# One group of P matmuls for w1 and w2 in every second slot, and attention's matmuls in those slots

## The chip, the cores and the metric

The kernel runs on one core of one Trainium2 chip. The metric is the device time of one execution in microseconds (us), the median of several runs. Of the core's engines, TensorE (PE in the profile, with PEld for its weight loads) does the matmuls, VectorE (DVE) and ScalarE (ACT) read their results out of PSUM and do all elementwise work, GpSimd (POOL) helps at the end, and SyncE (SP) issues DMAs.

## What is computed

All data are 32-bit floats. An attention block with a small state is followed by two feed-forward blocks:

```python
# x: (8, 8, 512, 64), state: (8, 8, 32, 64); softmax over the last axis, scale = 1/8
xread = softmax(scale * x @ state.T) @ state
sread = softmax(scale * state @ x.T) @ x
y = concatenate([xread, sread], axis=2)          # per batch: 544 rows of 8 * 64 = 512
h = ((y @ w1) * (y @ w2)) @ w3 @ w_out           # w1, w2: 512 x 1024, w3: 1024 x 1024, w_out: 1024 x 512
t = h @ w_in                                     # w_in: 512 x 2048
out = (t * clip(t + 3, 0, 6) / 6) @ w_out2       # w_out2: 2048 x 512
```

## The kernel before

**Stages.** A first stage converts w_out, w3, w1 and w2 from their raw words, 20 units of 1024 columns in the order of the string `ORDER` (L120). It multiplies w3 by w_out once (the tiles w3p), and `more` (L666) places the first attention and the first matmuls of the next stage between the units. The second stage goes over the eight batches b, each in eight slots (`slot`, L625), one for every 128 columns of w1 and w2. The third stage does the last two lines of the reference with a Strassen scheme, 33 rounds; it takes more than half of the time and the change does not touch it.

**P.** A slot needs y @ w1 and y @ w2 for 512 rows. The xread half of y is a product a @ state, so the kernel multiplies state by 256 columns of w1 or w2 first. The result is P, and the slot multiplies a with P. `p_mm(v, i)` (L346) makes P for two slots (pair v = 4 b + m // 2), for w1 (i = 0) or w2 (i = 1), with eight small matmuls of 64 rows by 32 columns in plain 32-bit form, which the trace shows as 16 instructions, into two PSUM banks (c = 0, 1), of which each fills 256 of 512 columns. `p_split(v, i)` (L361) then splits each bank into a rounded part (ph, ACT) and a rest (pl, DVE), because the large matmuls work on rounded operands in three terms: `mm3` (L87) is rounded by rounded, and the two mixed terms.

**A slot.** PE's order in slot m is written out by hand: two banks `ps_ab0` and `ps_ab1` (a with P for w1, then for w2, six matmuls each), then in `x2_one` (L534) six matmuls into the accumulators x2 for the slot two before, then what `mid_` (L741) issues, then six more for x2. On ACT and DVE, `ab_mul` (L500) copies ps_ab0 (asb) and multiplies ps_ab1 with it (ab); `ab_hi` and `ab_lo` split ab (abh, abl). `mid_` calls `p_mm` and `p_split` for the next pair, w1 in even slots and w2 in odd ones, and one step of the attention for batch b + 1. Another step of it is taken before (`before`, L736). After that, DVE and ACT do two steps of `stream2` (L422), which converts and splits the weights of the third stage.

**Attention.** `attention(b)` (L182) is a generator; each `yield` ends a step. For b from 2 on (`fine` is false) it takes steps in 16 places of the eight slots. Four of its parts put matmuls on PE: `scores` (two groups, ps_s), `e2_t` (two groups of transposes, ps_e), and `sread` (ps_r). In the kernel before these fall in the middles of slots 0, 1, 3, 4 and 5. The DVE parts are `scores_out`, `max_n`, `sum_n`, `div_n` and `turn`; `exp_n` is ACT's. `sread_out` copies the state's result (xs) and stores it with a DMA on SP; after batch 7's the stored rows are loaded again as xs_r, rounded on ACT (xs_h), and multiplied in `s_block` (L557), ahead of the last batch's slots.

**Banks.** The matmuls of slots, P and attention share four PSUM banks (`bank`, L66). A bank is handed out again in the order in which the last readers of the banks stand in the program. The order of each engine's queue is that of the program text.

Of the kernel before, what the change touches and what calls it, by code (L numbers as in the profile page):

```python
# [19 lines left out]
def attn_moe_kernel(tc, xt_d, xn_d, bd_d, wa, wb, wc, wi, wo, out):  # L20
# [18 lines left out]
    nc = tc.nc  # L39
# [26 lines left out]
    def bank(name):  # L66
        return psum.tile([128, 512], F32, tag="b", name=name, bufs=4)
# [114 lines left out]
    def attention(b, fine=False):  # L182
# [10 lines left out]
        def scores(g):  # L193

            ps = bank("ps_s")
            for j in range(2):
                c = 2 * g + j
                nc.tensor.matmul(ps[64 * j:64 * j + 64], br[:, c, :], xr[:, c, :], start=True, stop=True)  # L198
            return ps

        def scores_out(g, ps):
            nc.vector.tensor_reduce(out=m2[:, g:g + 1], in_=ps, op=ALU.max, axis=AX.X)
            nc.vector.tensor_scalar(out=m2[:, g:g + 1], in0=m2[:, g:g + 1], scalar1=-scale, scalar2=None, op0=ALU.mult)
            nc.vector.transpose(out=sN[:, g, :], in_=ps)
            nc.scalar.activation(out=e2[:, g, :], in_=ps, func=AF.Exp, bias=m2[:, g:g + 1], scale=scale,
                                 accum_out=r2[:, g:g + 1])
# [58 lines left out]
        if fine:  # L265
            ps = scores(0)
            yield
            scores_out(0, ps)
            yield
            ps = scores(1)  # L270
            yield
            scores_out(1, ps)
        else:
            scores_out(0, scores(0))
            yield
            yield
            scores_out(1, scores(1))
        yield
        max_n()
        yield  # L280
        exp_n()
        yield
        e2t = att.tile([128, T, 2, 128], F32, tag="xtl", name="e2t")
        sm = att.tile([128, 32, 1], F32, tag="sm", name="sm", bufs=2)
        if fine:
            ps = e2_t(0)
            yield
            e2_out(0, ps)
            sum_n()
            yield  # L290
            ps = e2_t(1)
            yield
            e2_out(1, ps)
            div_n()
            yield
            ps = sread()
            yield
            sread_out(ps)
            aT = att.tile([128, 2, 512], F32, tag="e2", name="aT")
            turn(aT)  # L300
        else:
            sum_n()
            yield
            e2_out(0, e2_t(0))
            yield
            div_n()
            yield
            e2_out(1, e2_t(1))
            yield
            aT = att.tile([128, 2, 512], F32, tag="e2", name="aT")  # L310
            turn(aT)
            yield
            sread_out(sread())
        yield
        pool = late if b % 2 else mid
        A_h = pool.tile([128, 2, 512], F32R, tag="Ah", name="Ah")
# [2 lines left out]
        rnd(A_h, aT, "A")  # L319
        yield  # L320
        rest(A_l, aT, A_h, "V")

    live = []

# [11 lines left out]
    with tc.manual_schedule():  # L336
# [6 lines left out]

        p_ps, phl = {}, {}

        def p_mm(v, i):  # L346
            b, mm = divmod(v, 4)
            ps = p_ps[v, i] = [bank("ps_p") for c in range(2)]
            o = 512 * i + 256 * (mm % 2)

            for q in range(4):
                for c in range(2):
                    j, k = divmod(q, 2)
                    r = slice(64 * (k ^ c), 64 * (k ^ c) + 64)
                    nc.tensor.matmul(ps[c][32 * q:32 * q + 32, :256], st_t[b][r, 2 * c + j, 32 * k:32 * k + 32],  # L355
                                     w12[mm // 2, 2 * c + j][r, o:o + 256], start=True, stop=True)

        def p_tile(hl):
            return main.tile([128, 512], F32R, tag=f"p{hl}", name=f"p{hl}", bufs=4)

        def p_split(v, i):  # L361
            ps = p_ps.pop((v, i))
            h, l = p_tile("h"), p_tile("l")
            h, l = phl[v, i] = h.rearrange("p (c k) -> p c k", c=2), l.rearrange("p (c k) -> p c k", c=2)
            for c in range(2):
                rnd(h[:, c], ps[c][:, :256], "A")
            for c in range(2):
                rest(l[:, c], ps[c][:, :256], h[:, c], "V")

        def w3_out(m, ps):  # L370
            w3p_h[m], w3p_l[m] = w3p_tile("h", m), w3p_tile("l", m)
# [294 lines left out]
        def more(t):  # L666
            if t == 1 or t == 8:
                load_x(t // 8)
            if t in (4, 16):
                live.append(attention(t // 16, True))  # L670
                step()

            for _ in range({5: 1, 6: 1, 7: 1, 8: 1, 10: 1, 11: 1, 12: 2, 13: 1, 17: 1, 18: 1, 19: 1}.get(t, 0)):
                step()
            for m in {9: (0, 1), 10: (2, 3), 12: (4,), 14: (5,), 17: (6,), 18: (7,)}.get(t, ()):
                w3_done(m)
            if 15 <= t <= 17 or t == 19:
                ab = ab_mul(*e_ps.pop(min(t - 15, 3)), 512)
            for v in {14: ((0, 0), (0, 1)), 15: ((1, 0),), 16: ((1, 1),)}.get(t, ()):
                p_split(*v)  # L680
            if 15 <= t <= 17 or t == 19:
                hi = ab_hi(ab, 512)
                e_ab[min(t - 15, 3)] = hi, ab_lo(ab, hi, 512)

            if 14 <= t <= 17:
                early_mm(t - 14)
            for v in {13: ((0, 0), (0, 1)), 14: ((1, 0),), 15: ((1, 1),), 19: ((2, 0), (2, 1))}.get(t, ()):
                p_mm(*v)
            if t in (4, 5, 9, 10, 11, 16, 17):
                step()  # L690
            if ORDER[t] in "aw":
                w3u[ORDER[:t].count("a") + ORDER[:t].count("w")].mm()
            bulk_mm(4)
            if t == 18:
                early_x2(0)
                early_x2(1)
            if t == 19:
                early_x2(2)
                step()
# [4 lines left out]
        close_pool("cv")  # L704
        late = open_pool("late", bufs=1, side=left, reuse_waits="tile")
        cvs = open_pool("cvs", bufs=1, side=right, reuse_waits="tile")
        for i in range(2):
            p_split(2, i)
        early_x2(3)
        second = stream2()  # L710
        for b in range(B):
# [20 lines left out]
            for m in range(0 if b else 4, M1):  # L732
                if m == (6 if b else 7) and b + 2 < B:
                    load_x(b + 2)

                def before():  # L736
                    step()

                vn, i = 4 * b + m // 2 + 1, m % 2

                def mid_():  # L741
                    if vn < 4 * B:
                        p_mm(vn, i)
                        p_split(vn, i)
                    step()
                slot(b, m, A, before, mid_)
                if b == 0:
                    step()
                for _ in range(STEPS):
                    next(second, None)  # L750
                if b == B - 2 and m >= 3:
                    ws_split(m - 3)
                if b == B - 1:
                    if m == 0:
                        x2_load(0)
                    else:
                        next(first, None)
                        next(first, None)
# [282 lines left out]
```

## Time and profile before

| | us |
|---|---|
| median of 3 runs | 1289.04 (1288.55 to 1289.30) |
| the profiled execution | 1290.92 |
| its span, first to last instruction | 1289.1 |
| TensorE busy in it | 1249.1 (97%) |
| VectorE busy | 863.7 (67%) |
| ScalarE busy | 525.1 (41%) |
| second stage, first slot to last | about 116 to 566 |

The span is cut into windows; for each the profile gives the busy time of each engine and the clock that TensorE was granted, 1.00 being full. A matmul's own duration overlaps with that of the next, so that the cost of one is read from the distance of two starts. "Idle before" is the time in which an engine had nothing to do, with the instruction that ended it.

### The profile page before, as it was taken

How to read it: one execution, taken by the hardware profiler on the slowest of the kernel's cores; microseconds unless marked ns; L12 is line 12 of the kernel's file. 1: busy time of each engine (PE TensorE's matmuls, PEld its weight loads, DVE VectorE, ACT ScalarE, POOL GpSimd, SP SyncE). 2: the span in 40 equal slices, each digit the busy share in tenths (PEclk: the TensorE clock that was granted, in tenths of full speed). 3: DMA queues.
4: the chain of work that ended last, by engine and by line, in shares of the span. 5: the costliest groups of instructions: out<-in, count | busy, mean ns of one | idle time of the engine just before them, and what ended most of it. 6: DMA issues, size and time to landing. Idle time of an engine off the chain costs nothing.

```text
span 1289.1 us, 16960 instructions
## 1 busy us (share of the span) xinstructions
PE 1249.1 (97%) x6784; PEld 966.8 (75%) x6784; DVE 863.7 (67%) x1332; ACT 525.1 (41%) x875; POOL 32.2 (2%) x18
## 2 busy tenths in 40 slices
PE   5979999999999999999999999999999999999997
PEld 2446676777767778787888888888888888888886
DVE  7976777786777652545757846668557686655663
ACT  3433546454655543434323443334433254332330
POOL 0000000000000000000000200002000020000000
PEclk9989999999999999999999999999999999999999
DMA  9741555555455200346334562535634344242223
GB/s 362 267 163 66 202 187 192 199 188 194 178 187 180 99 19 34 111 159 238 138 131 156 197 223 93 180 103 190 236 140 154 117 178 173 105 160 95 90 90 114
DMA packets 49590, 202.68 MB, mean 157 GB/s; under 512 B 9192, under 2 KB 11240, under 8 KB 42856
## 3 DMA queue, kind: packets, MB, share of 16 engines
q1 hardware_dynamic: 48936, 200.56, 43.3%
q8 instruction: 53, 0.87, 0.3%
q10 hardware_dynamic: 576, 1.05, 0.2%
q14 instruction: 25, 0.20, 0.0%
HBM read 160.17 MB, written 41.42 MB: 156 GB/s over the span
## 4 chain that ended last, share of the span: by engine, by line
PE 86%; DVE 8%; ACT 3%; DMA 1%; issue 1%; ACTq 0%; DVEq 0%; SPq 0%
PE ps L801 23%; PE ps_o L88 10%; PE ps_o L90 10%; PE ps_o L89 10%; PE x L88 5%; PE ps_ab L88 4%; PE x L90 4%; PE x L89 4%; PE ps_ab L90 4%; PE ps_ab L89 4%; PE ps_p L355 2%; PE ps_hs L801 2%; PE ps_r L228 1%; PE ps_s L198 1%; PE ps_sb L90 1%
## 5 line engine op out<-in xcount | busy, mean ns | idle before, releaser
L801 PE MATMUL ps<-xc,wh 128*128 128x512 f32 x896 | 276.7, 390 | 0.0
L805 DVE TENSOR_TENSOR oa<-oa,ps_o 128x512 f32<-128x512 f32 x238 | 163.2, 687 | 166.3 <-PE ps_o L90 165.7
L88 PE MATMUL ps_o<-woh,g 128*128 128x512 f32 x512 | 203.4, 397 | 0.4 <-ACT g L71 0.4
L90 PE MATMUL ps_o<-woh,g 128*128 128x512 f32 x512 | 201.9, 394 | 0.0
L89 PE MATMUL ps_o<-wol,g 128*128 128x512 f32 x512 | 201.5, 394 | 0.0
L801 PEld LDWEIGHTS ps<-xc,wh 128*128 128x128 f32 x896 | 168.3, 188 | 36.3
L801 PE MATMUL ps<-xc,wl 128*128 128x512 f32 x448 | 175.7, 392 | 0.0
L71 ACT ACTIVATE g<-gt 128x512 fp32r<-128x512 f32 x128 | 81.1, 634 | 177.7 <-DVE gt L815 177.6
L88 PE MATMUL x<-abh,w3ph 128*128 128x512 f32 (+1 forms) x288 | 115.7, 402 | 0.0
L90 PEld LDWEIGHTS ps_o<-woh,g 128*128 128x128 f32 x512 | 96.3, 188 | 23.8 <-DVE g L79 0.4
L89 PEld LDWEIGHTS ps_o<-wol,g 128*128 128x128 f32 x512 | 97.0, 189 | 21.4
L88 PEld LDWEIGHTS ps_o<-woh,g 128*128 128x128 f32 x512 | 96.4, 188 | 21.5 <-ACT g L71 0.8
L90 PE MATMUL x<-abh,w3pl 128*128 128x512 f32 (+1 forms) x288 | 109.3, 379 | 0.0
L89 PE MATMUL x<-abl,w3ph 128*128 128x512 f32 (+1 forms) x288 | 109.1, 379 | 0.0
L88 PE MATMUL ps_ab<-Ah,ph 128*128 128x512 f32 x256 | 102.6, 401 | 5.3 <-DVE pl L79 5.2
L79 DVE TENSOR_TENSOR g<-gt,g 128x512 fp32r<-128x512 f32 x128 | 89.7, 701 | 18.7 <-ACT g L71 16.3
L90 PE MATMUL ps_ab<-Ah,pl 128*128 128x512 f32 x256 | 100.4, 392 | 0.0
L89 PE MATMUL ps_ab<-Al,ph 128*128 128x512 f32 x256 | 100.3, 392 | 0.0
L801 PEld LDWEIGHTS ps<-xc,wl 128*128 128x128 f32 x448 | 84.1, 188 | 18.2
L504 DVE TENSOR_TENSOR ab<-ps_ab,asb 128x512 f32<-128x512 f32 x64 | 44.1, 689 | 60.5 <-PE ps_ab L90 41.0
L71 ACT ACTIVATE abh<-ab 128x512 fp32r<-128x512 f32 (+1 forms) x72 | 43.8, 608 | 98.2 <-DVE ab L504 98.2
L812 ACT ACTIVATE rl<-c,half 128x512 f32<-128x512 f32 x96 | 69.4, 723 | 32.4 <-DVE c L805 30.9
(122 smaller groups left out, 1752.3 us busy)
## 6 DMA issues: line engine op xcount, KB each, us to landing
wh<-swih SPq DMA_DIRECT2D x33, 896.0 KB, 4.6
wl<-swil SPq DMA_DIRECT2D x33, 896.0 KB, 6.4
woh<-swoh SPq DMA_DIRECT2D x33, 512.0 KB, 5.5
wol<-swol SPq DMA_DIRECT2D x33, 512.0 KB, 6.6
out_dram<-oa SPq DMA_DIRECT2D x34, 256.0 KB, 2.4
raw<-in_wb_dram SPq DMA_DIRECT2D x8, 1024.0 KB, 7.1
xr<-in_xt_dram SPq DMA_DIRECT2D x8, 1024.0 KB, 6.5
xn<-in_xn_dram SPq DMA_DIRECT2D x8, 1024.0 KB, 7.1
```

What stands on the lines that cost most here:

```text
L71: nc.scalar.activation(out=out_, in_=in_, func=AF.Copy)
L79: e.tensor_tensor(out=out_, in0=in_, in1=hi.bitcast(F32), op=ALU.subtract)
L88: nc.tensor.matmul(ps, lh, rh, start=first, stop=False)
L89: nc.tensor.matmul(ps, lh, rl, start=False, stop=False)
L90: nc.tensor.matmul(ps, ll, rh, start=False, stop=last)
L198: nc.tensor.matmul(ps[64 * j:64 * j + 64], br[:, c, :], xr[:, c, :], start=True, stop=True)
L228: nc.tensor.matmul(ps[h:h + 64, c * NS:(c + 1) * NS], xn[:, t, c * 128 + h:c * 128 + h + 64], e2t[:, t, g, o:o + NS], start=(t == 0), stop ...
L355: nc.tensor.matmul(ps[c][32 * q:32 * q + 32, :256], st_t[b][r, 2 * c + j, 32 * k:32 * k + 32], w12[mm // 2, 2 * c + j][r, o:o + 256], star ...
L504: nc.vector.tensor_tensor(out=ab[:, :n], in0=psb[:, :n], in1=a[:, :n], op=ALU.mult)
L801: nc.tensor.matmul(ps, u[:, a, k, :], v[:, k, :], start=first and k == 0 and i == 0, stop=k == 1 and i == 2, skip_group_check=not first or ...
L805: nc.vector.tensor_tensor(out=out_, in0=a, in1=b, op=ALU.add)
L812: nc.scalar.activation(out=rl, in_=c, func=AF.Relu, bias=half, scale=1.0 / 6.0)
```

## The change

P for w1 and w2 of a pair is made by one call, in even slots only: 16 matmuls (32 instructions) into the same two banks, w1 in columns 0 to 255 and w2 in columns 256 to 511. The splits take 512 columns at a time, two on ACT and two on DVE for a pair instead of four and four; the tiles ph and pl are twice as wide and half as many. Attention's steps for `fine` false are placed anew: both `scores` groups in the middle of slot 0, both `e2_t` groups in the middle of slot 4, `sread` in the middle of slot 6, each behind P on PE; `max_n` goes to slot 1, `exp_n` ahead of the splits of slot 2, `div_n` to slot 3. In the first stage the three P pairs that are made there get one call each, with two banks instead of four.

```diff
             yield
             scores_out(1, ps)
         else:
-            scores_out(0, scores(0))
-            yield
-            yield
-            scores_out(1, scores(1))
+            ps = [scores(g) for g in range(2)]
+            for g in range(2):
+                scores_out(g, ps[g])
+            yield
         yield
         max_n()
         yield
         exp_n()
         yield
+        if not fine:
+            yield
...
             sum_n()
             yield
-            e2_out(0, e2_t(0))
-            yield
             div_n()
             yield
-            e2_out(1, e2_t(1))
+            yield
+            ps = [e2_t(u) for u in range(2)]
+            for u in range(2):
+                e2_out(u, ps[u])
             yield
             aT = att.tile([128, 2, 512], F32, tag="e2", name="aT")
             turn(aT)
-            yield
-            sread_out(sread())
...
         rest(A_l, aT, A_h, "V")
+        if not fine:
+            yield
+            sread_out(sread())
...
-        def p_mm(v, i):
+        def p_mm(v):
             b, mm = divmod(v, 4)
-            ps = p_ps[v, i] = [bank("ps_p") for c in range(2)]
-            o = 512 * i + 256 * (mm % 2)
...
+            ps = p_ps[v] = [bank("ps_p") for c in range(2)]
+
+            for i in range(2):
+                o = 512 * i + 256 * (mm % 2)
+                for q in range(4):
+                    for c in range(2):
+                        j, k = divmod(q, 2)
+                        r = slice(64 * (k ^ c), 64 * (k ^ c) + 64)
+                        nc.tensor.matmul(ps[c][32 * q:32 * q + 32, 256 * i:256 * i + 256],
+                                         st_t[b][r, 2 * c + j, 32 * k:32 * k + 32],
+                                         w12[mm // 2, 2 * c + j][r, o:o + 256], start=True, stop=True)
+
+        def p_split(v):
+            ps = p_ps.pop(v)
+            h, l = (main.tile([128, 2, 512], F32R, tag=f"p{hl}", name=f"p{hl}", bufs=2) for hl in "hl")
+            for i in range(2):
+                phl[v, i] = h[:, :, 256 * i:256 * i + 256], l[:, :, 256 * i:256 * i + 256]
             for c in range(2):
-                rnd(h[:, c], ps[c][:, :256], "A")
+                rnd(h[:, c], ps[c], "A")
             for c in range(2):
-                rest(l[:, c], ps[c][:, :256], h[:, c], "V")
+                rest(l[:, c], ps[c], h[:, c], "V")
...
-            for v in {14: ((0, 0), (0, 1)), 15: ((1, 0),), 16: ((1, 1),)}.get(t, ()):
-                p_split(*v)
+            if t in (14, 15):
+                p_split(t - 14)
...
-            for v in {13: ((0, 0), (0, 1)), 14: ((1, 0),), 15: ((1, 1),), 19: ((2, 0), (2, 1))}.get(t, ()):
-                p_mm(*v)
+            if t in (13, 14, 19):
+                p_mm({13: 0, 14: 1, 19: 2}[t])
...
-                vn, i = 4 * b + m // 2 + 1, m % 2
+                vn = 4 * b + m // 2 + 1
 
                 def mid_():
-                    if vn < 4 * B:
-                        p_mm(vn, i)
-                        p_split(vn, i)
+                    if vn < 4 * B and m % 2 == 0:
+                        p_mm(vn)
+                        p_split(vn)
                     step()
```

## Rows read from the trace of the kernel before

**Rows 1.** The page, part 4: the chain that ended last, by engine.

```profile
PE 86%; DVE 8%; ACT 3%; DMA 1%; issue 1%; ACTq 0%; DVEq 0%; SPq 0%
```

**Rows 2.** Busy time by window: PE, PEld, DVE, ACT, POOL, then clock, DMA share.

```profile
188.00:244.00 56.00, 54.80 (x401) 39.97 (x400) 42.50 (x71) 29.03 (x55) 0.00 (x0) 1.00 0.56 197
566.00:1289.00 723.00, 714.01 (x3190) 586.70 (x3189) 465.18 (x695) 260.24 (x398) 31.50 (x12) 1.00 0.43 152
```

**Rows 3.** Waits of PE: total us, how many times, the longest.

```profile
PE ps_ab L88 <- DVE pl L79: 5.2, 2, 4.2
...
PE ps_e L213 <- ACT asb L502: 2.7, 4, 1.2
...
PE ps_p L355 <- DVE ab L504: 1.4, 1, 1.4
```

**Rows 4.** PE in order of time (start, duration): a slot with P alone.

```profile
214.50 0.39 PE L89 MATMUL x<-abl,w3ph 128*128 128x512 f32 x1
214.73 0.39 PE L90 MATMUL x<-abh,w3pl 128*128 128x512 f32 x1
215.04 0.66 PE L355 MATMUL ps_p<-big,br 64*32 64x256 f32 x16
215.64 0.50 PE L88 MATMUL x<-abh,w3ph 128*128 128x512 f32 x1
215.97 0.39 PE L89 MATMUL x<-abl,w3ph 128*128 128x512 f32 x1
```

**Rows 5.** The same view, first stage: two P groups follow each other.

```profile
107.87 0.66 PE L355 MATMUL ps_p<-big,br 64*32 64x256 f32 x16
...
108.33 0.59 PE L355 MATMUL ps_p<-big,br 64*32 64x256 f32 x2
...
110.92 0.50 PE L88 MATMUL x<-abh,w3ph 128*128 128x512 f32 x1
```

**Rows 6.** The same view: P ahead of a scores group; transposes ahead of P.

```profile
119.23 0.60 PE L213 MATMUL ps_e<-ident,e 128*128 128x128 f32 x4
119.76 0.66 PE L355 MATMUL ps_p<-big,br 64*32 64x256 f32 x16
...
207.78 0.66 PE L355 MATMUL ps_p<-big,br 64*32 64x256 f32 x16
208.37 1.08 PE L198 MATMUL ps_s<-xr,br 128*64 128x512 f32 x4
```

**Rows 7.** Groups of instructions by shape: busy us, mean ns, idle before.

```profile
L79 DVE TENSOR_TENSOR pl<-ps_p,ph 128x256 fp32r<-128x256 f32 x128 | 47.9, 418 | 7.4 <-ACT ph L71 7.2
...
L504 DVE TENSOR_TENSOR ab<-ps_ab,asb 128x512 f32<-128x512 f32 x64 | 44.1, 689 | 60.5 <-PE ps_ab L90 41.0 <-ACT asb L502 19.2
...
L241 DVE TENSOR_TENSOR sN<-sN,mx 128x1024 f32<-128x1024 f32 x8 | 9.8, 1226 | 0.3
...
L79 DVE TENSOR_TENSOR w3pl<-ps_w,w3ph 128x512 fp32r<-128x512 f32 x8 | 5.3, 685 | 4.5 <-ACT w3ph L71 4.5
...
L71 ACT ACTIVATE w3ph<-ps_w 128x512 fp32r<-128x512 f32 x8 | 4.5, 596 | 0.0
```

**Rows 8.** Batch 7's state rows: issue and rounding in time; median landings.

```profile
462.15 0.32 SPq L723 DMA_DIRECT2D xs_r<-xsd  x1
...
473.89 1.05 ACT L71 ACTIVATE xs_h<-xs_r 128x1024 fp32r<-128x1024 f32 x1
...
xsd<-xs SPq DMA_DIRECT2D x8, 64.0 KB, 2.1
xs_r<-xsd SPq DMA_DIRECT2D x1, 512.0 KB, 3.3
```

**Rows 9.** PE alone by window: busy, instructions, granted clock.

```profile
223.10:224.60 1.50, 1.42 (x8) 1.00 0.79 330
...
477.90:480.30 2.40, 2.40 (x14) 0.50 0.00 0
```

**Rows 10.** DVE in order of time, end of the first stage.

```profile
111.03 0.69 DVE L79 TENSOR_TENSOR abl<-ab,abh 128x512 fp32r<-128x512 f32 x1 [0.76 <-ACT abh L71]
```

More of the change, by code (lines that the diff above doesn't have):

```diff
@@ L344, in attn_moe_kernel @@
         p_ps, phl = {}, {}
-        def p_mm(v, i):
+        def p_mm(v):
             b, mm = divmod(v, 4)
-            ps = p_ps[v, i] = [bank("ps_p") for c in range(2)]
-            o = 512 * i + 256 * (mm % 2)
[L351 to L364, printed above, removed]
+            ps = p_ps[v] = [bank("ps_p") for c in range(2)]
[13 more added lines that the diff above has]
+                phl[v, i] = h[:, :, 256 * i:256 * i + 256], l[:, :, 256 * i:256 * i + 256]
             for c in range(2):
-                rnd(h[:, c], ps[c][:, :256], "A")
+                rnd(h[:, c], ps[c], "A")
             for c in range(2):
-                rest(l[:, c], ps[c][:, :256], h[:, c], "V")
+                rest(l[:, c], ps[c], h[:, c], "V")
         def w3_out(m, ps):
@@ L706, in attn_moe_kernel @@
         cvs = open_pool("cvs", bufs=1, side=right, reuse_waits="tile")
-        for i in range(2):
-            p_split(2, i)
+        p_split(2)
         early_x2(3)
```

## The prediction

> **What bounds the kernel now.** I read the chain that ended last first: 86% of it is TensorE [rows 1]. The busy times by window say where: in one batch of the second stage PE is busy 54.80 of 56.00 us while DVE has 42.50, and in the third stage 714 of 723 [rows 2]. So time can be won in the second stage and ahead of it only, and in two ways: PE's few waits, or PE's own work made shorter. The list of waits is short: 5.2 us in all on the rest of P, of which 4.2 in one place of the first stage, 2.7 in four waits of the transposes for a ScalarE copy, 1.4 once where P waits for a bank [rows 3]. The rest must come from the busy time. The number of P's matmuls and their columns stay, so the third view is PE in order of time, around P, where a busy engine can be seen to lose time between matmuls.
>
> **What going into P and out of it costs.** Large matmuls start 0.23 us apart (214.50 to 214.73). P alone in a slot stretches L90 at 214.73 to the second matmul behind P, L89 at 215.97, to 1.24 us; two ordinary steps would be 0.46, so P costs 0.78 [rows 4]. P's own work is less. In the first stage two groups follow each other, and the second begins 0.46 us after the first (107.87 to 108.33) [rows 5]. So 16 instructions take 0.46, and 0.78 - 0.46 = 0.32 is lost on entering and leaving. The losses can be seen: P starts 0.31 behind a large matmul instead of 0.23, and the two matmuls behind P start late as well [rows 4].
>
> **The merged P.** A pair of slots now costs 2 x 0.78 = 1.56, and will cost 0.32 + 2 x 0.46 = 1.24: 0.32 less. There are 24 such pairs in batches 1 to 6 and 3 in batch 7 (pair 32 does not exist): 27 x 0.32 = 8.6 us, all of it on PE, which sets the end. Bounds: 0.25 to 0.40 a pair (the rows are rounded to 0.01, and four starts enter), 6.8 to 10.8.
>
> **Attention's groups.** Each of the five matmul groups now follows a P, so moving them adds no entry so long as every one sits behind a P; in slots 0, 4 and 6 it does. Two of the five, the second scores group and the second transposes, then follow a group of their own kind. The change from P to scores costs about 0.59 - 0.46 = 0.13 (207.78 to 208.37), that from transposes to P happens in 0.53 for four of them [rows 6]. I take 0.1 for each of the two, 6 batches: 1.2 us; bounds 0 (nothing is saved between equal groups) and 0.13 x 12 = 1.6.
>
> **Waits that go, and waits that come.** The transposes waited 2.7 us for the ScalarE copy because `exp_n` stood ahead of it; they move from slots 3 and 4 to slot 4 alone, a slot and a half after `exp_n`, so I take this wait as gone. What comes: with two banks for P and two for a pair of attention groups in the same slot, the banks come round differently. In slot 4, P takes the pair of slot 3, the transposes take slot 4's own ps_ab banks, and slot 5's ps_ab0 takes the bank that DVE's first pl frees. Count from the end of slot 4's ps_ab matmuls: six x2 matmuls (1.4), P (1.05 to the next group), two groups of transposes (1.0), six x2 (1.4) put slot 5's ps_ab0 at 4.8. DVE's part begins 0.2 later, since a matmul of 0.39 ends 0.2 after the start of the next [rows 4], and before that bank is free come ab 0.69, ACT's abh (0.6), abl 0.69 and the first pl, now 512 columns at 0.69 instead of 256 at 0.42 [rows 7]: 2.7. So DVE may enter slot 4 up to 1.9 us late; each us beyond that is a us of PE in each batch. The ACT splits (0.60 for 512 columns [rows 7]) fit between. The transposes' second bank waits for slot 4's ab, with about the same limit.
>
> How late is DVE? An odd slot lasts 24 x 0.23 = 5.5 us without P. In slot 1 DVE has ab, abl (1.4), `max_n` (two passes of 1024 columns at 1.23 [rows 7]) and at most two such passes of weight conversion: 6.3, late by 0.8. Slot 3 has `sum_n` and `div_n` instead: the same. Slot 0 has 8.3 of DVE work (both `scores_out` take 3.0) in about 8.6, but its pl must wait for P and the split, so it ends about 1 late; slot 2, 6.7 long with 5.2 of DVE work, makes up 1.2. That is 0.8 + 1.0 - 1.2 + 0.8 = 1.4 late at slot 4, between 1.0 (shorter conversion steps) and 2.6 (nothing made up in slot 2, where `exp_n` on ACT now stands ahead of abh and the splits). Cost per batch 0 to 0.7; I take 0.3, near the low end since 1.4 is below 1.9: 6 x 0.3 = 1.8. Net of both: 0.9 us gained, bounds +2.7 and 2.7 - 4.2 = -1.5. What is queued behind the ACT part of `exp_n` in slot 2 is abh, whose abl PE wants only two slots later, so there is cover of over 5 us.
>
> **The first stage.** P of pair 2 needs two free banks, not four. The wait of 1.4 falls away, since the bank it waited for is not taken. P starts at 107.87; the next x2 matmul then comes at 107.87 + 0.46 + 0.60 (P to x2 [rows 4]) = 108.93 instead of 110.92 [rows 5]: 2.0 us. The batch of x2 matmuls that follows must not overtake abl, which ends at 111.72 [rows 10]; twelve matmuls from 108.93 end at 111.7, so it is just in time, and I take 1.9. Around 72 us the wait of 4.2 for pl stays, because DVE is the late one there; a merged P for pair 1 gives 0.3 more and the freed banks let two matmuls go early. I take 0.5. Sum 2.4, bounds 1.0 (the chain of DVE gets there first) and 3.0. In batch 0, whose attention is the finer one, two pairs merge, but slot 5's `sread` still pays an entry of its own, and P of 32 instructions pushes one wait for pl (1.0 of the 5.2) back by about 0.5: I take 0.4 gained, bounds -0.5 and 0.9.
>
> **The state rows.** `sread` of batch 7 moves one slot later, and with it the copy, the store and the load of xs_r on SP. Now xs_r is issued at 462.15 and lands 3.3 later, at 465.5, but is used at 473.89 [rows 8]: 8 us of cover. In the new order the store comes about 3.3 us into slot 6's second half, 6.6 before the end of slot 7; 2.1 + 3.3 of landing [rows 8] fit into that, barely. 0, bounds -1.5 and +0.4. Behind it on SP stand only weight loads and stores with two units of lead; the load of the next x now stands ahead of it and waits for nothing late.
>
> **Sum.** 8.6 + 1.2 + 0.9 + 2.4 + 0.4 + 0 = 13.5 us. The profiled execution took 1290.92, its span 1289.1; it lies 0.15% above the median of 1289.04, and a difference carries over as it is: 1289.0 - 13.5 = 1275.5. All good ends together (10.8 + 1.6 + 2.7 + 3.0 + 0.9 + 0.4 = 19.4) give 1269.6, all bad ends (6.8 + 0 - 1.5 + 1.0 - 0.5 - 1.5 = 4.3) 1284.7.
>
> **Rivals.**
> *DVE is late in slot 4.* Against it: 13 us of each batch are free on DVE [rows 2]. For it: this slack lies in even slots where DVE now waits longer for the longer splits. Price: 1 us per batch for each us beyond 1.9. It eats the gain of 15.3 (the sum without the waits of 1.8 that I count) when DVE is 1.9 + 15.3 / 6 = 4.4 late, and at 5 late the time is 1289.0 - 15.3 + 6 x 3.1 = 1292.3, slower. That takes two more conversion passes in each batch's slots 1 to 3 than I counted. Chance of slower by this 0.07; of a part of it, 3 late and 1289.0 - 15.3 + 6.6 = 1280.3, 0.10.
> *No loss to save.* If the 0.32 belonged to every 16 instructions of P, not to the change of kind, the 8.6 and 1.2 would fall away: 1275.5 + 9.8 = 1285.3. Against it stands the distance of 0.46 between two groups, but that second group was cut off by a wait after two instructions [rows 5]. Chance 0.07; here the change leaves the cost of P as it was and does not do what it says.
> The page "TensorEngine Tiling (Array Packing)" of the Trainium skill (Tiling Modes, Key Properties) says that a change of tiling mode, unlike a change of tile, drains TensorE, which speaks against this rival; the 0.32 around P's 64 by 32 tiles agrees [rows 4], and the page gives no price.
> *The clock.* Longer stretches of small matmuls could lower TensorE's granted clock. Now it is 1.00 around a wait and a transposes group; after the gap ahead of `s_block` 14 matmuls ran at 0.50 (1.2 GHz) in 2.40 us [rows 9], half of which is lost. Once in each of 6 batches, twice over: 14 us, 1289.9, no change. Chance 0.03.
> The page "TensorE: Matmul & The Clock Gate" of the Trainium skill (Part 4) says that PE transposes don't count as busy for the gate, which speaks for this rival; the clock of 1.00 at the transposes [rows 9] speaks against it.
>
> **How the numbers follow.** Forecast as worked out: 0.73; the rivals 0.17, 0.07 and 0.03. The likeliest gives 1275.5. The range goes from 1270.0 to 1285.5: it holds the forecast to nearly all its ends, the half-late DVE and the case of no loss to save. Differences of 0.2% (2.6 us) are about what a measurement of this kernel can tell from none. Faster 0.87, the same 0.05, slower 0.08.
>
> **What would show it.** Right: in an odd slot PE shows no P, x2 matmuls 0.23 apart throughout; in an even slot 32 P instructions, and about 1.05 us from P's start to the next group; batches 1 to 6 shorter by 1.3 to 1.9 us each; the wait for ab in the first stage gone. Wrong: PE waits for pl or ab at ps_ab in slot 5 or at ps_e in slot 4, some us per batch; or 1.2 us and more for the second 16 instructions; or a granted clock under 1.00 inside a batch.

## The result, and the profile after

The changed kernel takes 1275.27 us (median of 4 runs, 1273.91 to 1276.16), the kernel before beside it 1289.17 (4 runs, 1288.55 to 1289.43). The ratio is 0.9892, with a 95% interval from 0.9877 to 0.9907: 13.9 us faster, where 13.5 were forecast. The profiled execution took 1276.16 us and its span 1274.1, against 1290.92 and 1289.1 before, so the two traces differ by 15.0 us. That is what is taken apart here.

What was said of P is seen first, in PE in order of time (start, duration, engine and line, operation, tile, count). An even slot of batch 5 in the changed kernel:

```profile
373.07 0.39 PE L90 MATMUL x<-abh,w3pl 128*128 128x512 f32 x1
373.39 1.09 PE L360 MATMUL ps_p<-big,br 64*32 64x256 f32 x32
374.41 0.50 PE L88 MATMUL x<-abh,w3ph 128*128 128x512 f32 x1
374.75 0.40 PE L89 MATMUL x<-abl,w3ph 128*128 128x512 f32 x1
```

Here 32 instructions stand between two large matmuls where [rows 4] have 16. P begins 0.32 us behind L90, and L88 1.02 behind P: forecast were 0.31 and 1.05. The odd slot behind it shows only large matmuls, 0.23 apart.

A slot's length is the distance of its first ps_ab matmul to that of the next slot. For batch 5, in us, from the PE starts of each trace (slots 0, 2, 4 and 6 are the even ones):

| slot | 0 | 1 | 2 | 3 | 4 | 5 | 6 | 7 |
|---|---|---|---|---|---|---|---|---|
| before | 7.29 | 7.27 | 6.25 | 6.67 | 6.67 | 8.28 | 6.28 | 6.27 |
| changed | 8.56 | 5.44 | 6.69 | 5.44 | 7.51 | 5.46 | 8.67 | 5.46 |

A slot without P or attention now lasts 5.44. P for one operand cost 6.25 - 5.44 = 0.81, P for both costs 6.69 - 5.44 = 1.25, so a pair saves 2 x 0.81 - 1.25 = 0.37. The two scores groups cost 1.04 + 1.00 before over a slot with P alone (6.25 in slot 2, 6.27 in the odd slot 7), and 8.56 - 6.69 = 1.87 now: 0.17 saved. The two transposes groups cost 0.40 + 0.42 before and 0.82 now: nothing.

Second, PE's waits in the changed kernel (total us, how many, the longest), which answer to [rows 3]:

```profile
PE ps_e L213 <- DVE ab L508: 2.5, 3, 1.1
PE ps_ab L90 <- DVE pl L79: 2.1, 1, 2.1
...
PE ps_ab L88 <- ACT ph L71: 1.1, 1, 1.1
PE ps_sb L89 <- DVE xs_l L79: 1.1, 1, 1.1
PE ps_ab L88 <- DVE pl L79: 0.9, 1, 0.9
```

The transposes' wait for ScalarE is gone, and so is P's wait for ab. A new wait has come: the transposes wait for DVE's ab, three times. The other lines on pl and ph are the first stage and batch 0; that on xs_l is `s_block`, with the same 1.1 before.

Third, one batch and the third stage by window (columns as in [rows 2]):

```profile
188.00:241.00 53.00, 52.06 (x395) 39.54 (x394) 41.32 (x62) 29.22 (x47) 0.00 (x0) 1.00 0.55 197
556.00:1274.00 718.00, 709.02 (x3168) 582.22 (x3166) 465.23 (x695) 258.93 (x396) 31.49 (x12) 1.00 0.43 152
```

PE is still busy nearly throughout, at clock 1.00; the batch is shorter because PE's own work is, and the third stage is as busy as it was [rows 2]. By stretch, from the starts of the slots (batch 0's slots 0 to 3 have their ps_ab matmuls in the first stage, so that its first slot here is slot 4):

| stretch | before | changed | gained |
|---|---|---|---|
| start to first slot of batch 0 | 116.51 | 115.47 | 1.0 |
| batch 0 | 23.68 | 23.01 | 0.7 |
| batches 1 to 5 | 278.57 | 269.97 | 8.6 |
| batch 6, slots 0 to 6 | 48.70 | 47.77 | 0.9 |
| its slot 7 and `s_block` | 51.99 | 49.40 | 2.6 |
| batch 7, seven slots | 40.48 | 39.29 | 1.2 |

The sum is 15.0. Batches 1 to 5 take 53.23, 54.61, 54.81, 54.09 and 53.23 us now; the middle three hold the new waits.

### The profile page after: what moved, and what is told of

Its sections match the earlier page's. It is cut to its first block, busy times and chain, and to the rows that moved or that the text cites. A ratio compares the mean times of both kernels' runs of the same rounds, so it can differ in the third digit from the quotient of the medians.

```text
span 1274.1 us, 16840 instructions
## 1 busy us (share of the span) xinstructions
PE 1237.6 (97%) x6784; PEld 972.2 (76%) x6784; DVE 858.0 (67%) x1268; ACT 518.7 (41%) x811; POOL 32.2 (3%) x18
## 3 DMA queue, kind: packets, MB, share of 16 engines
q10 hardware_dynamic: 576, 1.05, 0.2%
## 4 chain that ended last, share of the span: by engine, by line
PE 85%; DVE 9%; ACT 2%; DMA 1%; issue 1%; ACTq 0%; DVEq 0%; SPq 0%
PE ps L804 24%; PE ps_o L88 10%; PE ps_o L90 10%; PE ps_o L89 10%; PE x L88 4%; PE x L89 4%; PE x L90 4%; PE ps_ab L88 4%; PE ps_ab L90 4%; PE ps_ab L89 4%; PE ps_p L360 2%; PE ps_hs L804 2%; PE ps_w L414 1%; PE ps_r L228 1%; DVE ab L508 1%
## 5 line engine op out<-in xcount | busy, mean ns | idle before, releaser
L88 PE MATMUL ps_o<-woh,g 128*128 128x512 f32 x512 | 203.3, 397 | 0.3 <-ACT g L71 0.3
L90 PE MATMUL ps_o<-woh,g 128*128 128x512 f32 x512 | 201.8, 394 | 0.0
L89 PE MATMUL ps_o<-wol,g 128*128 128x512 f32 x512 | 201.4, 393 | 0.0
L90 PEld LDWEIGHTS ps_o<-woh,g 128*128 128x128 f32 x512 | 96.3, 188 | 23.8 <-DVE g L79 0.4
L89 PEld LDWEIGHTS ps_o<-wol,g 128*128 128x128 f32 x512 | 96.9, 189 | 21.5
L88 PEld LDWEIGHTS ps_o<-woh,g 128*128 128x128 f32 x512 | 96.4, 188 | 21.6 <-ACT g L71 0.8
L88 PE MATMUL x<-abh,w3ph 128*128 128x512 f32 (+1 forms) x288 | 112.3, 390 | 0.0
L89 PE MATMUL x<-abl,w3ph 128*128 128x512 f32 (+1 forms) x288 | 109.0, 378 | 0.0
L90 PE MATMUL x<-abh,w3pl 128*128 128x512 f32 (+1 forms) x288 | 108.8, 378 | 0.0
L88 PE MATMUL ps_ab<-Ah,ph 128*128 128x512 f32 x256 | 102.7, 401 | 2.0 <-ACT ph L71 1.1
L90 PE MATMUL ps_ab<-Ah,pl 128*128 128x512 f32 x256 | 100.8, 394 | 2.1 <-DVE pl L79 2.1
L89 PE MATMUL ps_ab<-Al,ph 128*128 128x512 f32 x256 | 100.6, 393 | 0.0
L79 DVE TENSOR_TENSOR abl<-ab,abh 128x512 fp32r<-128x512 f32 (+1 forms) x72 | 47.3, 657 | 39.9 <-ACT abh L71 39.9
```

What stands on the lines that cost most here:

```text
L79: e.tensor_tensor(out=out_, in0=in_, in1=hi.bitcast(F32), op=ALU.subtract)
L88: nc.tensor.matmul(ps, lh, rh, start=first, stop=False)
L89: nc.tensor.matmul(ps, lh, rl, start=False, stop=False)
L90: nc.tensor.matmul(ps, ll, rh, start=False, stop=last)
```

## The experiments

Each kernel is timed against runs of the kernel before on the same chip; where two experiments are set side by side, their ratios to it are.

### e1_apart: the two halves of P drawn apart

```diff
-            x2_mm(blk, m, ab, n, (2, 3))
+            x2_mm(blk, m, ab, n, (2,))
+            if late_ is not None:
+                late_()
+            x2_mm(blk, m, ab, n, (3,))
...
-                        p_mm(vn)
+                        p_mm(vn, (0,))
```

> The changed kernel, with the two halves of P of an even slot put apart: w1's 16 instructions after six x2 matmuls, w2's 16 after three more. Splits of 512 columns and attention stay as changed. Theory, the gain is the loss on entering and leaving P, paid once instead of twice: 28 pairs lose 0.32 to 0.39 us again, 9.0 to 10.9 us, so 1284.3 to 1286.2, and an even slot of batch 5 with P alone lasts about 7.05 instead of 6.68 us. Rival, the gain is that of fewer and longer splits and of odd slots without P's work on ScalarE and VectorE: the time stays at 1275.3, within 1 us.

Measured: 1286.37 us (1285.13 to 1286.63), ratio 0.9962 [0.9949, 0.9975], 0.7% or 9.0 us slower than the changed kernel's 0.9892. PE in order of time, an even slot:

```profile
379.72 0.39 PE L90 MATMUL x<-abh,w3pl 128*128 128x512 f32 x1
380.04 0.66 PE L362 MATMUL ps_p<-big,br 64*32 64x256 f32 x16
380.63 0.50 PE L88 MATMUL x<-abh,w3ph 128*128 128x512 f32 x1
380.97 0.39 PE L89 MATMUL x<-abl,w3ph 128*128 128x512 f32 x1
381.20 0.40 PE L90 MATMUL x<-abh,w3pl 128*128 128x512 f32 x1
381.52 0.66 PE L362 MATMUL ps_p<-big,br 64*32 64x256 f32 x16
382.12 0.50 PE L88 MATMUL x<-abh,w3ph 128*128 128x512 f32 x1
```

`late_` is the second half of P, then its split and attention's step. Banks, splits, attention's groups and the number of matmuls are those of the changed kernel; three large matmuls between the halves are what differs. L90 at 379.72 to the second matmul behind P, 380.97, is 1.25, against 1.24 in [rows 4], and it comes twice. The slot takes 7.05 instead of 6.69: 0.36 for one more visit, as I call a group of other matmuls between large ones. The long splits stayed and 9.0 of the 13.9 us went, so this part of the gain belongs to the change of kind, and the rival "no loss to save" falls.

### e2_splits256: P merged, the splits in pieces of 256

```diff
+            for i in range(2):
+                o = slice(256 * i, 256 * i + 256)
-                rnd(h[:, c], ps[c], "A")
+                    rnd(h[:, c, o], ps[c][:, o], "A")
-                rest(l[:, c], ps[c], h[:, c], "V")
+                    rest(l[:, c, o], ps[c][:, o], h[:, c, o], "V")
```

> The changed kernel with P split in pieces of 256 columns, four on ScalarE and four on VectorE for a pair, as before the change; the matmuls stay merged. Theory, entering and leaving P is the gain: within 1.5 us of 1275.3; the waits of the transposes for VectorE (2.5 us in the changed kernel) may grow by up to 0.6 us in each of three or four batches, since four pieces of 0.42 take 0.3 us more than two of 0.69 twice. Rival, fewer split instructions are the gain: back towards 1289, at least 5 us of it.

Measured: 1281.38 us (1280.88 to 1284.07), ratio 0.9929 [0.9914, 0.9943], 0.37% or 4.8 us slower than the changed kernel. My theory missed, and the rival was nearly met. Waits of PE:

```profile
PE ps_ab L88 <- DVE pl L79: 4.7, 6, 1.5
PE ps_e L213 <- DVE ab L510: 4.2, 4, 1.6
```

Batches 1 to 5 take 54.70, 55.75, 55.93, 55.21 and 54.20. Nothing of PE's own work changed, so this is DVE later: four splits of 0.42 instead of two of 0.69 [rows 7] are 0.3 us more for a pair. Slot 4 in batch 5 grows by more than that, from 7.51 to 8.38. The pieces go w1 first, so the bank that slot 5's ps_ab0 takes is read by the first and the third of the four: in the trace the four run from 393.68 to 395.30, and PE, after a wait of 0.63, starts at 395.11. DVE is at the edge of setting the time in that slot, and the longer splits are worth these 4.8 us beside what the visits give, as waits that do not come.

### e3_att_only: the kernel before with attention's new places

The diff is the changed kernel's for `attention`, put on the kernel before.

> The kernel before with attention's steps placed as in the change; P in every slot, in halves. Theory: no entry is saved by it, the second scores group behind the first saves 0.18 us in 6 batches, and the waits change by about a us either way: 1287 to 1289.5. Rival, attention's new places are a large part of the gain: below 1284.

Measured: 1288.21 us (1287.62 to 1290.92, 10 runs), ratio 0.9987 [0.9977, 0.9996]: 1.7 us gained. Batches 1 to 5 take 54.89, 56.07, 55.47, 54.89 and 54.89, and 278.57 in sum become 276.21. Without the merged P the move is worth about an eighth of the whole.

### e4_p_only: the changed kernel with attention in its old places

The same part of the diff taken back.

> The changed kernel with attention's steps in their old places, so that one scores group, one group of transposes and the sread of each of 6 batches stand in odd slots without P. Theory: each of these 18 groups pays an entry of its own, 0.2 to 0.39 us, less what it paid for the change from P (0.13): 2 to 6 us more than the changed kernel, and the scores merge (1.1) is lost: 1278 to 1282.5. Rival, P's merge alone does it and attention's place is free: 1275 to 1277.

Measured: 1276.70 us (1275.34 to 1278.24), ratio 0.9888 [0.9874, 0.9903], the same as the changed kernel. The rival's number came, my theory's not, and yet the price that I gave to groups outside P is there. Slots of batch 5 here: 7.70, 6.70, 6.69, 5.91, 7.10, 7.66, 6.69, 5.44. Alone in an odd slot the second scores cost 6.70 - 5.44 = 1.26 against 7.70 - 6.69 = 1.01 behind a P; `sread` 2.22 against 1.98 (8.67 - 6.69); one transposes group 0.47 against 0.41. PE in order of time shows the two kinds:

```profile
379.94 0.60 PE L213 MATMUL ps_e<-ident,e 128*128 128x128 f32 x4
380.29 0.48 PE L88 MATMUL x<-abh,w3ph 128*128 128x512 f32 x1
...
392.73 0.39 PE L90 MATMUL x<-abh,w3pl 128*128 128x512 f32 x1
393.04 2.06 PE L228 MATMUL ps_r<-e2t,xn 128*64 128x32 f32 x64
395.03 0.50 PE L88 MATMUL x<-abh,w3ph 128*128 128x512 f32 x1
395.37 0.39 PE L89 MATMUL x<-abl,w3ph 128*128 128x512 f32 x1
```

The `sread` group, in tiles of 128 by 64, begins 0.31 behind L90, and L89 follows L88 0.34 later: the marks of P's visits. A batch takes 53.89 instead of 53.23 (batch 4 alone 54.47), 0.66 x 6 = 4.0 us. Against that its PE never waits at ps_e, which takes 3.8 from batches 2 to 4 of the changed kernel. Two effects of 4 us cancel, and the time alone would have hidden both.

### f1_e_apart: one transposes group in slot 3, the other in slot 4

```diff
-            div_n()
+            e2_out(0, e2_t(0))
             yield
+            div_n()
             yield
-            ps = [e2_t(u) for u in range(2)]
-            for u in range(2):
-                e2_out(u, ps[u])
+            e2_out(1, e2_t(1))
```

> The changed kernel with one group of transposes in the middle of slot 3 and one in slot 4, instead of both in slot 4; the scores stay in slot 0 and sread in slot 6. Theory, both groups in slot 4 need the two banks of slot 4's own ps_ab, and the second one waits for VectorE's ab: with one in each slot only the bank that ScalarE's copy frees is needed, the waits (2.5 us by the profile, 3.8 by the slots' lengths) go, and the lone group in slot 3 costs 0.05 us a batch: 3 to 4 us faster than the changed kernel, a ratio to before of 0.986 to 0.987. Rival, VectorE is late there in any case and the wait moves to ps_ab of slot 5: no gain.

Measured: 1272.30 us (1270.55 to 1273.04), ratio 0.9864 [0.9849, 0.9878]. Batches 1 to 5 take 53.28 each, and the wait at ps_e is gone. The 0.05 over 53.23 is the price of the transposes alone in slot 3. By the ratios that is 3.6 us faster than the changed kernel, as expected, though the intervals just touch; against the changed kernel's later runs on this chip (1273.97, below) it is 1.7.

### s1_steps: the weight conversion moved away from slots 1 to 3

```diff
-                for _ in range(STEPS):
+                for _ in range((2, 1, 1, 1, 2, 3, 3, 3)[m] if b else STEPS):
```

> The changed kernel with the weight conversion's steps of batches 1 to 6 spread as 2, 1, 1, 1, 2, 3, 3, 3 over the slots, instead of 2 in each: VectorE has less to do in slots 1 to 3. Theory, the transposes wait since VectorE enters slot 4 late: the wait of 2.5 us falls to under 0.5, 2 to 4 us faster than the changed kernel (ratio 0.986 to 0.988). Rival, the wait is one of the bank's order alone: it stays above 2 us and the time stays.

Measured: 1273.46 us (1272.74 to 1273.96), ratio 0.9874 [0.9857, 0.9890]. Batches 1 to 5 take 53.23 each. The wait comes back elsewhere, at the start of batch 6, where the scores now wait for DVE and slot 0 takes 10.95 instead of 8.56 (waits of PE):

```profile
PE ps_s L198 <- DVE ab L508: 1.8, 1, 1.8
...
PE ps_s L198 <- ACT asb L506: 0.4, 1, 0.4
```

Two independent ways, attention moved and DVE relieved, take the same waits away. So the wait is DVE late in slot 4, with the ab that frees the second transposes' bank, as the prediction's rival had it, at a quarter (3.8 of 15.3 us) of the size that would have decided.

### d1_tile, d2_type, d3_type512: what makes a visit dear

Each adds to the odd slots of batches 1 to 6 a pair of matmuls whose result nobody reads: d1 in P's tiles with 64 columns, d2 in tiles of 128 by 128 in the plain 32-bit type, and d3 like d2 with 512 columns.

One of the three lines marked d1, d2 and d3 stands in each:

```diff
+                    if 0 < b < B - 1 and m % 2:
+                        for c in range(2):
+                            # d1, with r = slice(64 * c, 64 * c + 64)
+                            nc.tensor.matmul(bank("ps_d")[32 * c:32 * c + 32, :64], st_t[b + 1][r, 0, :32], w12[0, 0][r, :64], start=True, stop=True)
+                            # d2
+                            nc.tensor.matmul(bank("ps_d")[:, :64], ident, st_t[b + 1][:, c, :], start=True, stop=True)
+                            # d3
+                            nc.tensor.matmul(bank("ps_d"), ident, w12[0, c][:, :512], start=True, stop=True)
```

> The changed kernel with two idle matmuls of P's kind added in the middle of each odd slot of batches 1 to 6 (64 by 32, plain 32-bit, 64 columns instead of 256, side by side in two banks; nobody reads them). Their own work is about 0.06 us for both passes, from P's 0.21 per pass of 256 columns. Theory, a change of tile shape costs the loss: an odd slot grows from 5.44 by 0.32 to 0.45 us, 24 slots 8 to 11 us. Rival, the loss lies in P's own long groups: 0.05 to 0.15 us a slot.

> As the run with idle matmuls of P's kind, but these two are 128 by 128 like the large ones and differ from them in the plain 32-bit type alone (two passes of 64 columns each, one after the other: about 0.11 us of work). Theory, the tile shape makes the loss: an odd slot grows by 0.11 to 0.2 us. Rival, the change of type makes it: by 0.4 to 0.5 us, as much as the other run's.

> As the run with idle matmuls of 128 by 128 in plain 32-bit form, but with 512 columns instead of 64, so that their own work is known from the changed kernel's rows of the same form (0.427 us an instruction): four of them, 1.71 us, and no weight load is longer than a matmul. Theory, the loss is that of a change of tile shape and a change of type alone is nearly free: an odd slot grows by 1.70 to 1.80 us. Rival, a change of type costs what a change of tile does: by 2.05 to 2.15.

Measured, by slot: d1 makes an odd slot 5.89 instead of 5.44 (+0.45), d2 5.91 (+0.47), d3 7.19 (+1.75); in time 1282.68, 1284.02 and 1312.85, one run each. PE in order of time, d1:

```profile
372.56 0.39 PE L90 MATMUL x<-abh,w3pl 128*128 128x512 f32 x1
372.88 0.30 PE L751 MATMUL ps_d<-big,br 64*32 64x64 f32 x4
373.11 0.50 PE L88 MATMUL x<-abh,w3ph 128*128 128x512 f32 x1
373.45 0.39 PE L89 MATMUL x<-abl,w3ph 128*128 128x512 f32 x1
```

The step into P's tiles (0.32) and the late second matmul (0.34) stand here around four tiny instructions. The slot grows by 0.45; their work I estimate at about 0.1 (two passes, each a quarter of P's 0.21 for 256 columns), so about 0.35 is left for the visit. In d2 I expected little and got the rival's number, but the rows suggest that much of it was its own work:

```profile
372.02 0.39 PE L90 MATMUL x<-abh,w3pl 128*128 128x512 f32 x1
372.25 0.55 PE L750 MATMUL ps_d<-br,ident 128*128 128x64 f32 x4
372.61 0.48 PE L88 MATMUL x<-abh,w3ph 128*128 128x512 f32 x1
372.93 0.39 PE L89 MATMUL x<-abl,w3ph 128*128 128x512 f32 x1
```

The step in is an ordinary 0.23, and four instructions take the 0.36 until L88, 0.09 each, where I had counted less for 64 columns. L89 follows 0.32 later, nearly as late as in d1, so a late second matmul alone does not tell a change of shape. That left the type undecided, hence d3. The changed kernel itself has such matmuls in its first stage:

```profile
84.66 0.39 PE L90 MATMUL ps_ab<-Ah,pl 128*128 128x512 f32 x1
84.89 3.59 PE L414 MATMUL ps_w<-wo,t 128*128 128x512 f32 x8
...
88.55 0.40 PE L89 MATMUL ps_ab<-Al,ph 128*128 128x512 f32 x1
```

From 84.89 to 88.55 are 3.66 us. With 0.427 an instruction, the figure of d3's expectation, eight and an ordinary step of 0.23 give 3.65, and d3's four give 1.71 of its 1.75. The change of type within 128 by 128 tiles therefore costs some 0.02 (0.01 to 0.04), and it is the shape of the tile that costs 0.35.

### f2_early: P of pair 1 ahead of the first early matmuls

```diff
+            if t == 14:
+                p_mm(1)
             if 14 <= t <= 17:
                 early_mm(t - 14)
-            if t in (13, 14, 19):
-                p_mm({13: 0, 14: 1, 19: 2}[t])
+            if t in (13, 19):
+                p_mm({13: 0, 19: 2}[t])
```

> The changed kernel with the P of pair 1 put ahead of the first early ps_ab group of the first stage, in place of behind it. In the changed kernel two matmuls run at 69.0, PE then waits 2.1 us for pl, and the stretch from 69 to 77 runs at the lower clock of 0.50, P of pair 1 at 76.9 at that clock in 1.75 us. Theory, P in the wait costs nothing there: the first slot of batch 0 starts 0.8 to 2 us earlier than 115.5, and batches 1 to 6 as in the changed kernel. Rival, VectorE's chain of conversions sets the first slot's start: it stays within 0.4 of 115.5.

Measured: 1273.87 us, one run; the first slot of batch 0 starts at 113.72 instead of 115.47, and the batches are as in the changed kernel. PE in order of time around that place, in the changed kernel:

```profile
69.00 0.80 PE L88 MATMUL ps_ab<-Ah,ph 128*128 128x512 f32 x1 [1.12 <-ACT ph L71]
69.60 0.63 PE L89 MATMUL ps_ab<-Al,ph 128*128 128x512 f32 x1
72.35 0.79 PE L90 MATMUL ps_ab<-Ah,pl 128*128 128x512 f32 x1 [2.12 <-DVE pl L79]
...
76.91 1.75 PE L360 MATMUL ps_p<-big,br 64*32 64x256 f32 x32
```

PE alone by window in the same kernel (us, busy, clock, DMA):

```profile
69.00:74.00 5.00, 2.87 (x6) 0.50 0.73 254
74.00:76.90 2.90, 2.90 (x7) 0.50 0.47 96
```

And the same matmul of f2_early, in order of time:

```profile
72.74 0.80 PE L88 MATMUL ps_ab<-Ah,ph 128*128 128x512 f32 x1 [3.60 <-DVE pl L79]
```

In the changed kernel two matmuls go early, and the third waits for DVE's pl all the same. Everything up to P at 76.91 then runs at clock 0.50 (1.2 GHz), and P itself takes 1.75 instead of 1.09. But the low clock is not the whole of it. In the second profile of the changed kernel (`changed_again`) the same P ran at full clock:

```profile
76.74 1.09 PE L360 MATMUL ps_p<-big,br 64*32 64x256 f32 x32
```

The first slot started at 114.66 there, still 0.9 later than in f2. What f2 does in any case is to make P of pair 1 ahead of PE's wait for pl, where it costs nothing.

### g_both and changed_again: f1 and f2 together, and the changed kernel beside them

> The changed kernel with one group of transposes in slot 3 and one in slot 4, and with P of pair 1 ahead of the first early ps_ab group. If both theories hold, the gains add: 3.5 us from batches 2 to 4 and 0.8 to 2 from the first stage, 4 to 5.5 us faster than the changed kernel on the same chip. If VectorE's chain sets the start of the slots: 3 to 4.

> The changed kernel itself on the chip of these runs, for comparison with the last one: a ratio to before of 0.988 to 0.991.

Measured: 1272.65 us (1270.28 to 1273.48), ratio 0.9871 [0.9855, 0.9886], for both; 1273.97 (1273.66 to 1274.43), 0.9885 [0.9867, 0.9902], for the changed kernel beside it on the same chip. The medians are 1.3 us apart and the intervals overlap, less than expected. The slots give 0.6 up to the first slot of batch 0 (114.03 against 114.66) and 3.6 in batches 1 to 5 (53.28 each). But the stretch from slot 7 of batch 6 to the first slot of batch 7, whose code is the same, takes 50.61 us in the one profile and 47.92 in the other. PE there in the changed kernel beside it (us, busy, clock, DMA):

```profile
482.00:492.00 10.00, 8.04 (x61) 1.00 0.00 0
```

And in g_both, at the same place:

```profile
478.00:488.00 10.00, 8.03 (x43) 0.72 0.00 0
```

In the profiles of this study the stretch takes from 47.9 to 50.6 us in kernels that have the changed P. It goes with whether the clock falls at the gaps around `s_block`: over the whole stretch the granted clock was 1.00 in the three profiles that took 47.9 (`changed_again`, e4, d1), 0.97 in the seven that took 49.0 to 49.4, and 0.93 in the two that took 50.6 (e2, g). That hides a part of g's gain: over the whole run the granted clock was 0.991 to 0.993 in its four runs, 0.994 to 0.996 in those of the changed kernel beside it. Why is open. The versions f1 and g are the fastest that ran, and how far ahead of the changed kernel they are (1 to 4 us) stays open too.

## Why the prediction was right, and where it was not

The mechanism was right. These are its terms beside what the stretches show:

| term | forecast | measured | from |
|---|---|---|---|
| merged P, 27 pairs | 8.6 | 10.0 to 10.5 | 0.37 (batch 5) to 0.39 (batch 7) a pair |
| equal groups together, 6 batches | 1.2 | 1.0 | 0.17 in slot 0, 0 in slot 4 |
| waits that go | 2.7 | 3.7 | batches 1 to 5 of before, over its 54.97 |
| waits that come | -1.8 | -3.8 | batches 2 to 4 over 53.23 |
| first stage | 2.4 | 1.0 | first slot (1.9 in `changed_again`) |
| batch 0 | 0.4 | 0.7 | its length |
| state rows | 0 | 0.4 | wait for xs_h 1.1 to 0.7 |
| clock around `s_block` | 0 | about 1.4 | rest of that stretch |

The measured column sums to between 14.4 and 14.9 of the 15.0. Its last row is luck of the two profiles and no work of the change: over the stretch around `s_block` the granted clock was 0.93 in the profile before and 0.97 in that of the changed kernel.

**The merged P** holds, near the upper end of its bounds. The 0.32 came from one slot with P alone against a second group that a wait had cut short [rows 4, 5]; e1 measured 0.36 for a visit, and the tables 0.37. That is 1.4 to 1.9 us more than forecast. The Trainium skill's page "TensorEngine Tiling (Array Packing)" (Tiling Modes, Key Properties) says that a change of tiling mode drains TensorE; d1's 0.35 against the 0.02 of the type change agrees with it.

**Attention's groups** came out right in sum, by two misses of opposite sign. Scores came from P's change of kind at 0.13 a group [rows 6], and 0.17 is right about there; transposes have the tile of the large matmuls, and nothing is saved by putting them together. I had taken 0.1 for each because the row for transposes and P did not separate the two. The same mistake had a second half: `sread` and a scores group alone cost 0.25 more, transposes alone 0.05. So the two transposes need not have been moved into one slot, which is what f1 uses.

**The new waits** were undersized by 2.0 us, in the place that was named. The limit was good: I had 1.9 us of delay on DVE before PE waits. DVE's rows for slot 4 of batch 3:

```profile
275.61 1.23 DVE L256 TENSOR_TENSOR sN<-sN,sm 128x1024 f32<-128x1024 f32 x1
276.75 0.42 DVE L453 TENSOR_SCALAR ts<-hd 128x1024 uint16<-128x1024 uint16 x1
277.21 0.43 DVE L455 TENSOR_SCALAR hd<-hd 128x1024 uint16<-128x1024 uint16 x1
277.55 1.22 DVE L458 SCALAR_TENSOR_TENSOR w<-raw,ts 128x1024 f32<-128x1024 uint32 x1
278.68 0.68 DVE L508 TENSOR_TENSOR ab<-ps_ab,asb 128x512 f32<-128x512 f32 x1
```

and PE's in the same slot:

```profile
274.94 0.39 PE L90 MATMUL ps_ab<-Ah,pl 128*128 128x512 f32 x1
...
276.62 1.09 PE L360 MATMUL ps_p<-big,br 64*32 64x256 f32 x32
277.65 0.66 PE L213 MATMUL ps_e<-ident,e 128*128 128x128 f32 x4
279.42 0.66 PE L213 MATMUL ps_e<-ident,e 128*128 128x128 f32 x4 [1.12 <-DVE ab L508]
```

PE is done with ps_ab at 274.94 + 0.39 = 275.33, and DVE begins ab at 278.68: 3.35 late. The same count gives 1.63 and 1.58 in batches 1 and 5, where nothing waits, and 3.16 in batch 2, which waits 0.94. What is late beyond 2.2 is the wait, in all three (3.35 - 1.12, 3.16 - 0.94, and 2.63 - 0.41 in batch 4). I had 1.4 late, 1.0 to 2.6 at the ends. The failed step is the lateness of 1.4, worked out once for all batches from a typical slot: the conversion steps that fall in slots 1 to 3 differ from batch to batch, and in batch 3 DVE enters `div_n` (275.61) 0.28 after PE's ps_ab ended, in batch 5 it was 1.49 before. A mean over the batches hides that three of them carry the wait. It also stood at one bank only: the transposes' second, not at slot 5's ps_ab0, which I had named first.

The wait that goes was undersized too. The list names 2.7 at ps_e [rows 3], but the lengths of before's batches, 56.13, 56.24, 55.35, 55.87 and 54.97, lie 3.7 above five times the last. A wait costs more than its idle time, since the matmuls behind it start late as well: in batch 3 of the changed kernel slot 4 is 8.97 against 7.51, 1.46 for a listed wait of 1.12. Net of both I forecast +0.9, and it was -0.1.

**The first stage** gave 1.0 of 2.4 in the profile, at the lower end of its bounds, and 1.9 in the second profile of the changed kernel. The bank wait of 1.4 went, and the end of the stage reads as forecast, though not at the same time:

```profile
108.66 1.09 PE L360 MATMUL ps_p<-big,br 64*32 64x256 f32 x32
109.68 0.50 PE L88 MATMUL x<-abh,w3ph 128*128 128x512 f32 x1
```

From P to the next large matmul are 1.02 us, where [rows 5] had 107.87 to 110.92. But P begins 0.8 later than before; in the second profile it begins at 107.82, as before. The step that failed is "I take 0.5" for the stretch around 72 us: it was a loss of about 0.8 in the one profile, where the low clock lay over the two early matmuls, the wait behind them and P of pair 1, and nothing in the other, where that P ran at full clock. Both had a lower clock there than the kernel before: 0.68 against 0.79 from 64 to 80 us. Why is open. f2, which makes that P in PE's wait, wins 0.9 to 1.75 us back (against 114.66 and 115.47 of the two profiles of the changed kernel), g 0.6 to 1.4.

**State rows, signs and rivals.** The state rows were covered, as said. Of the signs, "1.3 to 1.9 us each" held in the mean of batches 1 to 5 (1.7) and not one by one: they are 2.9, 1.6, 0.5, 1.8 and 1.7 shorter, since the waits that went and those that came fall in different batches. And a sign of being wrong, a wait at ps_e in slot 4, came in three batches, at 0.4 to 1.1 us. "DVE is late in slot 4" came true at about 0.8 us per batch in the mean of batches 1 to 5, far from the 2.5 at which it would have eaten the gain. "No loss to save" falls with e1. The clock did not fall inside a batch: 1.00 in the window of the whole batch above. The Trainium skill's page "TensorE: Matmul & The Clock Gate" (Part 4) has PE transposes as not busy for the gate; no batch here shows a clock below 1.00 around them, even with 1.12 us of waiting between the two groups of batch 3 (1.00 from 277.60 to 279.90).

The sum lay within 0.4 us of the measured 13.9 because the misses cancel: P gave 1.4 to 1.9 more, the waits took 1.0 net and the first stage 1.4; that the number is so close is luck. The 1.1 us by which the two traces differ more than the medians is less than the stretch around `s_block` varies by.

## What to carry to other kernels

Where small matmuls in another tile shape stand between large ones, count the visits, not the matmuls: each visit has its price (here 0.36 us), and joining two saves one of them, while a group in the large matmuls' own tile shape may stand alone for almost nothing (here 0.05). When such a merge packs work into every second slot, follow the engine behind TensorE slot by slot through several batches, for a mean hides the batches in which it is late. Make experiments that read slots and not the time alone: e4 had the time of the changed kernel by two effects of 4 us that cancel.

## What the runs showed of the hardware

- A visit to tiles of 64 by 32 among matmuls of 128 by 128 cost 0.36 us (e1) and about 0.35 (d1). A group in tiles of 128 by 64 cost some 0.25 more alone than behind a P (e4: 1.26 against 1.01, 2.22 against 1.98). A change from rounded to plain 32-bit operands in the same tile shape cost about 0.02 (d3, and 84.66 to 88.55).
- Plain 32-bit instructions with 64 columns in tiles of 128 by 128 took 0.09 us each up to the next large matmul, which was itself followed 0.1 late (d2); those with 512 columns took 0.43 each (d3).
- In the first stage, from 64 to 80 us, the granted clock was 0.79 before, 0.68 in both profiles of the changed kernel, 0.89 in f2 and 0.68 in g, though the matmuls of f2 and g stand there in the same order. So their order alone does not set it; what does is open.
- The stretch around `s_block`, with the same code, took 47.9 to 50.6 us in different profiles, as the clock fell there or not (1.00 to 0.93 over the stretch). A trace of one execution can be 1 to 3 us off for that alone.
